# Windowed attention with a gated MLP on one core: second heads of blocks 0 to 2 scaled by GpSimd, first two weight chunks loaded and converted earlier

## The chip, the cores and the metric

One NeuronCore of a Trainium2 chip runs the whole program. The metric is device time in microseconds (us) of one execution; the figure of the kernel before is the median of three runs. A profiled execution of the same program gives the rows that are read below.

## The reference

Inputs are q, k, v of shape (4, 8, 768, 64), two integers n_global (8) and n_local (96), and the weights w_in (512 x 2048) and w_out (2048 x 512). q, k and v are 32-bit floats; the weights come as 64-bit floats and are brought to 32 bits on the chip.

```python
scores = scale * q @ k.T + bias                  # bias = -slope[head] * distance
scores = where(is_global | is_local, scores, -1e9)
a = exp(scores - max(scores)); a = a / (sum(a) + 1e-9)
x = (a @ v) -> (3072, 512)                       # heads side by side
h = x @ w_in;  g = h * sigmoid(h);  out = g @ w_out
```

A query sees the first 8 keys and the 96 keys up to its own position, so a block of 128 queries needs 232 keys: 96 of the block before, 8 global ones, 128 of its own (the first block of each batch needs its own 128 alone).

## The kernel before, in words

**Attention** goes by 24 blocks of 128 queries (4 batches of 6). A block has 4 *pairs* of heads; pair u = 4 * block + hp counts them through. For each pair: TensorE (PE) makes the scores (L625; two pairs in one go in blocks 0 to 5); VectorE (DVE) adds the bias and takes the row maximum, once for each head (L638); ScalarE (ACT) takes the exponential and its row sum (L646); DVE guards and inverts the sum (L653, L657); each head's row is multiplied by the inverse (`norm`, L662 to L668; called *scaling* here); PE turns the rows (L682); ACT moves the turned rows out of PSUM (L692); when the four pairs of a block are there, PE multiplies them with v (L707), ACT casts the result to the high part of x (L725) and DVE takes the low part (L728). In blocks 0 to 2 (pairs 0 to 11) DVE scales both heads of a pair; in pairs 12 to 23 ACT scales the second head (`on_act`, L659, `NA=(12, 24)`).

**The MLP** takes two blocks as a *group* (12 groups). In groups 0 and 1 it goes by 16 steps f: PE makes h (L868, 12 matmuls of 256 columns, of xh and xl with the high and low parts of w_in), ACT and DVE make the gate and its high and low parts (L874, L878, L882, L886), PE multiplies with w_out (L893, 6 matmuls of 512 columns). From group 2 on two steps go together (L971, L1040), by another scheme that the change does not touch.

**The weights** come as 32 chunks n, w_in for even n and w_out for odd n, so that step f needs the chunks 2f and 2f+1. A chunk is loaded by a DMA on SyncE's queue (SP; `stage`, L413), put together from the halves of the 64-bit numbers by three DVE instructions (`conv1` to `conv3`, L415, L421, L427), cast to its high part by ACT (`conv_hi`, L439), and DVE takes the low part (`conv_lo`, L443). The result of the odd chunks also goes back to DRAM from SP's queue (L436).

**The order** is the result of a planner that runs when the kernel is built (`Plan.run`, L102). Every piece of work has an engine, a cost estimate, a *rank*, the pieces that it waits for, and the buffers that it takes. The planner walks through time and gives each free engine the ready piece of the lowest rank. Each engine then executes its list in that order and waits for whatever is not there. In attention, rank is about the pair's number; chunk n is converted at rank `C0 + CR * n` = 14 + n and its load is at one rank less (L447, L449). GpSimd (POOL) has little to do at first: in blocks 0 to 5 it copies columns of k from block to block (L610, L612), and one bias (L339).

Of the kernel before, what the change touches and what calls it, by code (L numbers as in the profile page):

```python
# [17 lines left out]
ALU = mybir.AluOpType  # L18
# [16 lines left out]

    C0=14, CR=1, LW=1, LB=5, QB=3.5, RI=2.8, RN=2.8, RP=0.2, RM=0, RV=1.2, RQ=0.1, RB=3, LK=-25, LAG=1,

    BP=(4, 3), NX=20, CF=8, AHEAD=5, SB=(4,), LQ=(1, 2), CN=3, I0=6, QS='ACT', G0=2, TR=10, RL=4500, TL=6000, CL=3200, VC=8, WT=2, TP=3, ORD=(5, 7, 0, 1, 2, 3, 4, 6), NA=(12, 24), V2=6,
)


# [143 lines left out]
def attn_moe(ctx, tc, q, k, v, n_global, n_local, w_in, w_out, out):  # L185
    nc = tc.nc
# [257 lines left out]

    o_w, o_l, o_raw, o_st = [], [None, None], [], []
    for n in range(2 * NFC):
        rank = PAR["C0"] + PAR["CR"] * n  # L447
        a, m, x = [] if lent(n) is not None else [Buf("big")], Buf("mid", "m"), lent(n)
        o = op("DMA", 1456, rank - PAR["LW"], (lambda n=n: stage(n, "w")), [o_l[x]] if not a else (), a, PAR["DW"])  # L449
        o_st.append(o)  # L450
        o = op("DVE", 335, rank, (lambda n=n: conv1(n)), [o], [*a, m])
        o = op("DVE", 602, rank, (lambda n=n: conv2(n)), [o], [*a, m])
        o = op("DVE", 602, rank, (lambda n=n: conv3(n)), [o], [*a, m])
        if x is not None:
            o_l[x] = o
        o_wf = o
        if n % 2:
            o_raw.append(op("DMA", 800, rank, (lambda n=n: keep_raw(n)), [o], [m], PAR["DO"]))
        hi = op("ACT", 520, rank, (lambda n=n: conv_hi(n)), [o] + (o_l if n >= 2 * NFC - 4 else []), [m])
        lo = op("DVE", 602, rank, (lambda n=n: conv_lo(n)), [hi], [m])  # L460
        o_w.append((hi, lo))
# [197 lines left out]
    def on_act(u):  # L659
        return (1,) if PAR["NA"][0] <= u < PAR["NA"][1] else ()  # L660

    def norm(i, hp, a):  # L662
        t = blk[i]
        x = t["p", hp][:, a, :cols(i)[1]]
        if a in on_act(NHP * i + hp):
            nc.scalar.mul(x, x, t["inv", hp][:, a:a + 1])
        else:
            nc.vector.tensor_scalar(x, x, t["inv", hp][:, a:a + 1], None, ALU.mult)  # L668
# [71 lines left out]
    for i in range(B * NJ):  # L740
# [60 lines left out]
        for hp in range(NHP):  # L801
            u = NHP * i + hp
            stacked = i >= PAR["I0"]
            kind = pt_kind(i, hp)
            pe, pt, tp = Buf("pe", "m"), Buf(kind, "m" if kind == "pt" else None), Buf("tp")
            n = cols(i)[1]
            hps = (hp,) if stacked or (not i and hp < 2) else (hp - hp % 2, hp - hp % 2 + 1)
            if hp == hps[0]:
                s = [Buf("s") for _ in range(1 if stacked else 2)]
                ks = [kk[x] for x in (("KH", "KL", "QH", "QL", "R") if stacked else ("KH", "QH"))]  # L810
                before["s"] = o_s[u] = op(
                    "PE", 440 if stacked else 390 + len(hps) * (385 if j else 218), u,
                    (lambda i=i, hps=hps, s=s: stack_scores(i, hps[0], s) if i >= PAR["I0"] else scores(i, hps, s)),
                    [x for y, x in ob.items() if i or y[1] <= hps[-1] < y[2]] + [before.get("s")], s + ks,
                )
            o = before["s"]
            if not u:
                for x in later:
                    plan.after(x, o)
            if u == PAR["HU"] - 1:  # L820
                o["hold"] = 1
            o_e = []
            for a in range(2):
                x = op("DVE", 318 if j else 210, u, (lambda i=i, hp=hp, a=a: top_of(i, hp, a)),
                       [o, o_b[j == 0, hp], before.get("top") if not a else None], [s[a % len(s)], pe])
                if not a:
                    before["top"] = x
                o_e.append(op("ACT", ACT(n, 112) + 186, u, (lambda i=i, hp=hp, a=a: expo(i, hp, a)), [x], [pe]))
            if i >= PAR["VC"] and hp == 1:
                o_c.append(op("DVE", 598, u + 0.5, (lambda i=i: check_here(i)), [arrived, before["top"]], [kk["vn"]]))  # L830
            o = op("DVE", 67, u - PAR["RI"], (lambda i=i, hp=hp: guard(i, hp)), o_e, [pe])
            o = op("DVE", 72, u - PAR["RI"], (lambda i=i, hp=hp: inverse(i, hp)), [o], [pe])
            o = [op(*(("ACT", ACT(n)) if a in on_act(u) else ("DVE", 250 if j else 196)), u - PAR["RN"], (lambda i=i, hp=hp, a=a: norm(i, hp, a)), [o], [pe])
                 for a in range(2)]
            o = op("PE", 438 if j else 220, u - PAR["RP"], (lambda i=i, hp=hp, tp=tp: turn_p(i, hp, tp)), [*o, joint], [pe, tp])
            o_m.append(op("ACT", ACT(512 if j else 256), u - PAR["RM"], (lambda i=i, hp=hp, pt=pt: move_p(i, hp, pt)), [o, before.get("move")], [tp, pt]))
            before["move"] = o_m[-1]
            pts.append(pt)
# [660 lines left out]
```

## Time and profile before

| what | value |
|---|---|
| runs | 672.61, 673.05, 673.12 us; median 673.05 |
| profiled execution | 673.47 us, of which the span of the trace is 671.7 |
| PE, DVE, ACT, POOL busy | 99%, 81%, 64%, 23% of the span |
| granted TensorE clock | 1.00 of full speed in every slice |
| chain that ended last | PE 94%, DVE 5%, ACT 1% |

The shares of the span are an average over stages. The first 45 us, in which attention runs ahead and the first weights are converted, look different from the rest: there PE has gaps and DVE or ACT hardly any. So the table to read first is the one by stretches of time, and after it each engine's instructions in order of time around the places where PE waits.

### The profile page before, as it was taken

How to read it: one execution, taken by the hardware profiler on the slowest of the kernel's cores; microseconds unless marked ns; L12 is line 12 of the kernel's file. 1: busy time of each engine (PE TensorE's matmuls, PEld its weight loads, DVE VectorE, ACT ScalarE, POOL GpSimd, SP SyncE). 2: the span in 40 equal slices, each digit the busy share in tenths (PEclk: the TensorE clock that was granted, in tenths of full speed). 3: DMA queues.
4: the chain of work that ended last, by engine and by line, in shares of the span. 5: the costliest groups of instructions: out<-in, count | busy, mean ns of one | idle time of the engine just before them, and what ended most of it. 6: DMA issues, size and time to landing. Idle time of an engine off the chain costs nothing.

```text
span 671.7 us, 15715 instructions
## 1 busy us (share of the span) xinstructions
PE 662.1 (99%) x5756; PEld 635.6 (95%) x5756; DVE 543.9 (81%) x1501; ACT 432.2 (64%) x1026; POOL 156.2 (23%) x345
## 2 busy tenths in 40 slices
PE   8999999999999999999999999999999999999997
PEld 6788999899999999999999999999999999999997
DVE  6999999998668888878878878877879887975545
ACT  6997544687567676665775766674767666663332
POOL 2100000010003322324323323323332322332331
PEclk9999999999999999999999999999999999999999
DMA  9997757575887589669577677675876788744451
GB/s 183 223 292 246 235 165 232 180 236 181 237 248 249 167 261 280 199 178 297 190 222 237 196 213 219 206 234 171 281 220 191 224 229 212 234 161 153 129 190 34
DMA packets 146067, 141.62 MB, mean 211 GB/s; under 512 B 88356, under 2 KB 115492, under 8 KB 145988
## 3 DMA queue, kind: packets, MB, share of 16 engines
q1 hardware_dynamic: 145984, 140.60, 70.3%
q8 instruction: 46, 0.75, 0.5%
q14 instruction: 33, 0.27, 0.1%
q10 hardware_dynamic: 4, 0.00, 0.0%
HBM read 117.44 MB, written 18.87 MB: 203 GB/s over the span
## 4 chain that ended last, share of the span: by engine, by line
PE 94%; DVE 5%; ACT 1%; issue 0%; DVEq 0%; ACTq 0%
PE bank L971 33%; PE bank L1040 29%; PE bank L893 7%; PE bank L868 6%; PE bank L707 5%; PE bank L682 5%; PE bank L595 5%; PE bank L527 3%; DVE pe L638 1%; DVE pe L668 1%; PE bank L625 1%; PE bank L1312 0%; ACT pe L646 0%; DVE wf L427 0%; DVE wf L421 0%; DVE ost L1072 0%
## 5 line engine op out<-in xcount | busy, mean ns | idle before, releaser
L989 POOL TENSOR_TENSOR sg<-sg 128x128 f32<-128x128 f32 x285 | 131.1, 481 | 285.3 <-DVE sg L983 232.5
L971 PE MATMUL bank<-xh,WIH 128*128 128x256 f32 x640 | 183.2, 286 | 0.0
L971 PE MATMUL bank<-xl,WIH 128*128 128x256 f32 x640 | 177.9, 278 | 0.0
L971 PE MATMUL bank<-xh,WIL 128*128 128x256 f32 x640 | 177.7, 278 | 0.0
L1011 DVE TENSOR_TENSOR gl<-sg,gh 128x512 fp32r<-128x512 f32 (+1 forms) x152 | 98.2, 651 | 37.9 <-ACT gh L1005 34.1
L971 PEld LDWEIGHTS bank<-xl,WIH 128*128 128x128 f32 x640 | 120.7, 189 | 0.5
L971 PEld LDWEIGHTS bank<-xh,WIH 128*128 128x128 f32 x640 | 120.7, 189 | 0.4
L971 PEld LDWEIGHTS bank<-xh,WIL 128*128 128x128 f32 x640 | 120.4, 188 | 0.0
L1005 ACT CAST gh<-sg 128x512 fp32r<-128x512 f32 (+1 forms) x152 | 84.0, 568 | 54.1 <-PE bank L1040 40.3
L646 ACT ACTIVATE pe<-pe,NM 128x232 f32<-128x232 f32 (+1 forms) x192 | 90.2, 473 | 36.7 <-DVE NM L638 35.9
L977 ACT ACTIVATE sg<-bank 128x512 f32<-128x512 f32 x80 | 47.7, 597 | 47.8 <-PE bank L971 47.3
L638 DVE CUSTOM_DVE_ANT_0 pe<-bank,B 128x232 f32<-128x232 f32 (+1 forms) x192 | 66.6, 374 | 12.8 <-PE bank L595 11.7
L1040 PE MATMUL bank<-WOH,gh 128*128 128x256 f32 (+1 forms) x280 | 73.8, 295 | 0.0
L983 DVE SCALAR_TENSOR_TENSOR sg<-sg,bank 128x512 f32<-128x512 f32 x80 | 54.8, 685 | 23.5 <-ACT sg L977 22.9
L1040 PE MATMUL bank<-WOL,gh 128*128 128x256 f32 (+1 forms) x280 | 72.3, 289 | 0.0
L668 DVE TENSOR_SCALAR pe<-pe,sm 128x232 f32<-128x232 f32 (+1 forms) x180 | 60.5, 371 | 1.4
L682 PE MATMUL bank<-ident,pe 128*128 128x128 f32 (+1 forms) x352 | 55.0, 276 | 3.7 <-DVE pe L668 3.5
L692 ACT COPY pt<-bank 128x512 f32<-128x512 f32 (+1 forms) x82 | 44.7, 549 | 15.5 <-PE bank L682 13.4
L1040 PEld LDWEIGHTS bank<-WOH,gh 128*128 128x128 f32 x280 | 52.8, 189 | 1.5 <-issue 0.7
L1040 PEld LDWEIGHTS bank<-WOL,gh 128*128 128x128 f32 x280 | 52.7, 188 | 0.8
L1040 PE MATMUL bank<-WOH,gl 128*128 128x256 f32 (+1 forms) x280 | 49.0, 292 | 0.0
L682 PEld LDWEIGHTS bank<-ident,pe 128*128 128x128 f32 (+1 forms) x352 | 39.9, 136 | 9.0 <-DVE pe L668 6.1
(165 smaller groups left out, 1511.0 us busy)
## 6 DMA issues: line engine op xcount, KB each, us to landing
tx<-ts SPq DMA_DIRECT2D x72, 512.0 KB
ty<-ts SPq DMA_DIRECT2D x72, 256.0 KB
c<-in_moe_w_in_dram SPq DMA_DIRECT2D x16, 512.0 KB
c<-in_moe_w_out_dram SPq DMA_DIRECT2D x16, 512.0 KB
vn<-in_v_dram SPq DMA_DIRECT2D x24, 256.0 KB
w<-in_moe_w_in_dram SPq DMA_DIRECT2D x12, 512.0 KB
w<-in_moe_w_out_dram SPq DMA_DIRECT2D x12, 512.0 KB
kn<-in_k_dram SPq DMA_DIRECT2D x23, 256.0 KB
```

What stands on the lines that cost most here:

```text
L638: nc.vector.tensor_tensor_reduce(t["p", hp][:, a, :n], t["s", hp][a][:, :n], B1[:, hp] if i % NJ else B0[:, hp], -SC / (1 + a), 3.0e38, AL ...
L646: nc.scalar.activation(x, x, AF.Exp, bias=NM[:, i * H + h:i * H + h + 1], scale=-1.0, accum_out=t["sum", hp][:, a:a + 1],)
L668: nc.vector.tensor_scalar(x, x, t["inv", hp][:, a:a + 1], None, ALU.mult)
L682: nc.tensor.transpose(ps[:n, c, a], pe[:, a, c0:c0 + n], ident)
L893: nc.tensor.matmul(po, a[:, s], w_o(w, f), start=f == 0 and n == 0, stop=f == NFC - 1 and n == 2)
L971: nc.tensor.matmul(ph[:, a], w[:, cc, fs], x[:, cc], start=not cc and not m, stop=cc == NCC - 1 and m == 2)
L977: nc.scalar.activation(x[:, 0:4].rearrange("p (a b) c -> p a (b c)", a=2), mo["ph", g, n], AF.Tanh, scale=0.5)
L983: nc.vector.scalar_tensor_tensor(x, x, 1.0, mo["ph", g, n], ALU.add, ALU.mult)
L989: (eng.tensor_sub if e else eng.tensor_add)(x[:, o], x[:, a], x[:, b])
L1005: nc.scalar.copy(mo["gh", g, n][:, a:b], mo["sg", g, n][:, a + o:b + o])
L1011: nc.vector.tensor_sub(mo["gl", g, n][:, a:b], mo["sg", g, n][:, a + o:b + o], mo["gh", g, n][:, a:b].bitcast(F32))
L1040: nc.tensor.matmul(o, l, r, start=(g, b) not in opened, stop=n == NFC // 2 - 1 and m == 2 and (p in ((2, 7, 5, 4) if g == NGRP - 1 else (6 ...
```

## The change

It does two things. First, in pairs 0 to 11 the second head (a = 1) is scaled by GpSimd instead of DVE, with a planner cost of 450 (128 keys) or 650 (232 keys). Second, chunks 0 and 1 get ranks of their own: the load is at rank 0.3 (before: 13 and 14) and the conversion at rank 8 and 8.1 (before: 14 and 15); rank 8 is where pair 8, the first of block 2, stands. All other ranks stay, and lines behind L660 move down by 1 to 5. The number of instructions on PE stays.

```diff
-    BP=(4, 3), NX=20, CF=8, AHEAD=5, SB=(4,), LQ=(1, 2), CN=3, I0=6, QS='ACT', G0=2, TR=10, RL=4500, TL=6000, CL=3200, VC=8, WT=2, TP=3, ORD=(5, 7, 0, 1, 2, 3, 4, 6), NA=(12, 24), V2=6,
+    BP=(4, 3), NX=20, CF=8, AHEAD=5, SB=(4,), LQ=(1, 2), CN=3, I0=6, QS='ACT', G0=2, TR=10, RL=4500, TL=6000, CL=3200, VC=8, WT=2, CE=8, LE=0.3, NP=(0, 12), TP=3, ORD=(5, 7, 0, 1, 2, 3, 4, 6), NA=(12, 24), V2=6,
...
-        rank = PAR["C0"] + PAR["CR"] * n
+        rank = PAR["C0"] + PAR["CR"] * n if n > 1 else PAR["CE"] + n / 10
...
-        o = op("DMA", 1456, rank - PAR["LW"], (lambda n=n: stage(n, "w")), [o_l[x]] if not a else (), a, PAR["DW"])
+        o = op("DMA", 1456, rank - PAR["LW"] if n > 1 else PAR["LE"], (lambda n=n: stage(n, "w")), [o_l[x]] if not a else (), a, PAR["DW"])
...
+    def on_pool(u, a):
+        return a == 1 and PAR["NP"][0] <= u < PAR["NP"][1]
+
     def norm(i, hp, a):
         t = blk[i]
         x = t["p", hp][:, a, :cols(i)[1]]
-        if a in on_act(NHP * i + hp):
+        if on_pool(NHP * i + hp, a):
+            nc.gpsimd.tensor_scalar(x, x, t["inv", hp][:, a:a + 1], None, ALU.mult)
+        elif a in on_act(NHP * i + hp):
...
-            o = [op(*(("ACT", ACT(n)) if a in on_act(u) else ("DVE", 250 if j else 196)), u - PAR["RN"], (lambda i=i, hp=hp, a=a: norm(i, hp, a)), [o], [pe])
+            o = [op(*(("POOL", 650 if j else 450) if on_pool(u, a) else ("ACT", ACT(n)) if a in on_act(u) else ("DVE", 250 if j else 196)), u - PAR["RN"], (lambda i=i, hp=hp, a=a: norm(i, hp, a)), [o], [pe])
```

The planner makes a new order of it on every engine. It differs from the old one in the first stage alone: from the middle of group 2 on, PE's order is the same row for row. Three places matter to what follows.

SP's queue, from the q of block 2 on. kn, qn and vn are the loads of k, q and v of a block (kn_307 and kn_379 are block 3's, vn_394 and vn_393 block 2's, qn_351 and qn_415 block 3's), vp what a block keeps of the block before. Before:

```order
L513 DMA qn_287<-in_q_dram 128x8x64
L513 DMA kn_307<-in_k_dram 128x8x64
L521 DMA vp_333<-vn_232 96x512
L522 DMA vp_333<-vp_274 8x512
L513 DMA qn_351<-in_q_dram 128x8x64
L513 DMA kn_378<-in_k_dram 128x8x64
L513 DMA vn_394<-in_v_dram 128x8x64
```

And with the change:

```order
L513 DMA qn_287<-in_q_dram 128x8x64
L411 DMA w_0_309<-in_moe_w_in_dram 128x4x256
L411 DMA w_1_340<-in_moe_w_out_dram 128x1024
L521 DMA vp_367<-vn_232 96x512
L522 DMA vp_367<-vp_274 8x512
L513 DMA kn_379<-in_k_dram 128x8x64
L513 DMA vn_393<-in_v_dram 128x8x64
L513 DMA qn_415<-in_q_dram 128x8x64
```

The two chunks stand ahead of the k of block 3, and the q of block 3 now stands behind the v of block 2, which waits until block 0 is done with its buffer.

ACT's queue up to the cast of block 3's result (xh_616 from bank4_113 before, xh_649 from bank1_110 now; it makes group 1 ready). wf are converted chunks on the way to their high part, ths and ghs the gate of a step f and its high part, pe the rows of a pair. Before:

```order
L882 CAST ghs_125<-ths0_127 128x256
L600 ACTIVATE QHw_695<-bank2_111,few_121 128x512
L692 COPY pt_700<-bank1_110 128x512
L439 CAST WIH_104<-wf_2_653 128x4x128
L646 ACTIVATE pe_702,sm_703<-pe_702,NM_108 128x232 x2
L646 ACTIVATE pe_731,sm_732<-pe_731,NM_108 128x232 x2
L666 ACTIVATE pe_702<-pe_702,sm_703 128x232
L725 CAST xh_616<-bank4_113 128x4x128
```

And with the change:

```order
L697 COPY pt_729<-bank0_109 128x512
L600 ACTIVATE QHw_734<-bank7_116,few_121 128x512
L439 CAST WOH_106<-wf_3_674 128x512
L879 ACTIVATE ths0_127<-bank2_111 128x256
L671 ACTIVATE pe_687<-pe_687,sm_688 128x232
L646 ACTIVATE pe_719,sm_720<-pe_719,NM_108 128x232 x2
L887 CAST ghs_125<-ths0_127 128x256
L730 CAST xh_649<-bank1_110 128x4x128
```

Chunk 3's high part (before: the row behind the cast of block 3), the gate of step 1 and its high part now stand ahead of it; all else that ACT does up to there is the same in number.

PE's queue at the first matmul of group 1 (the row that reads xh_616 before, xh_649 now). Before, with the rows of pair 17 (pe_731) just turned:

```order
L682 MATMUL bank0_109<-ident_99,pe_731 104x128 x2
L682 MATMUL bank0_109<-ident_99,pe_731 128x128 x2
L868 MATMUL bank3_112<-xh_391,WIH_104 128x256
L868 MATMUL bank3_112<-xl_400,WIH_104 128x256
L868 MATMUL bank3_112<-xh_391,WIL_105 128x256
L868 MATMUL bank3_112<-xh_391,WIH_104 128x256
L868 MATMUL bank3_112<-xl_400,WIH_104 128x256
L868 MATMUL bank3_112<-xh_391,WIL_105 128x256
L868 MATMUL bank4_113<-xh_616,WIH_104 128x256
```

And with the change, where pair 17 is pe_719:

```order
L898 MATMUL bank3_112<-WOH_106,ghs_125 128x512
L898 MATMUL bank3_112<-WOL_107,ghs_125 128x512
L898 MATMUL bank3_112<-WOH_106,gls_126 128x512
L873 MATMUL bank7_116<-xh_649,WIH_104 128x256
L873 MATMUL bank7_116<-xl_665,WIH_104 128x256
L873 MATMUL bank7_116<-xh_649,WIL_105 128x256
L873 MATMUL bank7_116<-xh_649,WIH_104 128x256
L873 MATMUL bank7_116<-xl_665,WIH_104 128x256
L873 MATMUL bank7_116<-xh_649,WIL_105 128x256
L687 MATMUL bank2_111<-ident_99,pe_719 104x128 x2
```

Up to the turn of pair 17 PE had 18 matmuls L868 and 3 L893 of group 0 before; up to group 1's first matmul it now has 24 and 9, while pair 17 is turned behind it. The rest of what lies ahead is the same in number.

## Rows read from the trace of the kernel before

**Rows 1.** Stretches of time: start and end, length, busy us by engine, clock, DMA.

```profile
core 0: us, PE busy (x) PEld busy (x) DVE busy (x) ACT busy (x) POOL busy (x), PEclk, DMA share, GB/s
0.00:10.70 10.70, 9.35 (x46) 7.27 (x47) 5.78 (x33) 4.76 (x12) 2.84 (x15) 1.00 0.92 169
10.70:28.00 17.30, 16.21 (x154) 12.91 (x155) 15.33 (x90) 17.18 (x61) 2.04 (x6) 1.00 0.87 207
28.00:44.10 16.10, 13.50 (x138) 10.87 (x136) 16.07 (x60) 15.66 (x47) 1.17 (x2) 1.00 1.02 276
44.10:662.00 617.90, 617.90 (x5386) 599.75 (x5384) 501.44 (x1309) 392.08 (x905) 148.90 (x320) 1.00 0.70 212
662.00:671.70 9.70, 5.14 (x43) 4.75 (x41) 5.28 (x13) 2.50 (x5) 1.29 (x2) 1.00 0.18 57
```

**Rows 2.** Chain that ended last, around 78 us: start, length, work.

```profile
77.73 2.09 PE bank L893 x9
79.82 1.41 PE bank L868 x12
```

**Rows 3.** Instructions in order of time, PE: start, length, what; turn of pair 17.

```profile
44.87 0.81 PE L682 MATMUL bank<-ident,pe 128*104 128x128 f32 x4
45.43 0.36 PE L868 MATMUL bank<-xh,WIH 128*128 128x256 f32 x1
```

**Rows 4.** In order of time, DVE: low part of block 3's result.

```profile
44.55 0.71 DVE L728 TENSOR_TENSOR xl<-bank,xh 128x512 fp32r<-128x512 f32 x1
```

**Rows 5.** In order of time, ACT: four rows back to back.

```profile
47.42 0.62 ACT L439 CAST WIH<-wf 128x512 fp32r<-128x512 f32 x1
47.94 0.40 ACT L882 CAST ghs<-ths 128x256 fp32r<-128x256 f32 x1
48.25 0.37 ACT L874 ACTIVATE ths<-bank 128x256 f32<-128x256 f32 x1
48.52 0.48 ACT L666 ACTIVATE pe<-pe,sm 128x232 f32<-128x232 f32 x1
```

**Rows 6.** In order of time, DVE: conversion and scaling back to back.

```profile
36.27 0.40 DVE L415 TENSOR_SCALAR wf<-w 128x512 uint32<-128x512 uint32 x1
36.60 0.33 DVE L668 TENSOR_SCALAR pe<-pe,sm 128x232 f32<-128x232 f32 x1
36.85 0.67 DVE L443 TENSOR_TENSOR WOL<-wf,WOH 128x512 fp32r<-128x512 f32 x1
37.45 0.15 DVE L653 TENSOR_SCALAR sm<-sm 128x2 f32<-128x2 f32 x1
```

**Rows 7.** In order of time, POOL: a bias, and a copy without DVE conversions beside it.

```profile
6.85 0.56 POOL L339 TENSOR_SCALAR B<-t 128x128 bf16<-128x128 f32 x1 [4.63 <-DVE t L314]
...
13.04 0.21 POOL L610 COPY KHw<-KHw 128x32 f32<-128x32 f32 x1 [0.91 <-PE bank L625]
```

**Rows 8.** In order of time, POOL: copies with DVE conversions beside them.

```profile
29.78 0.72 POOL L610 COPY KHw<-KHw 128x32 f32<-128x32 f32 x1 [6.95 <-PE bank L625]
30.45 0.50 POOL L612 COPY KHw<-KHw 128x384 f32<-128x384 f32 x1
```

**Rows 9.** In order of time, DVE: the conversions beside those copies.

```profile
29.74 0.69 DVE L421 SCALAR_TENSOR_TENSOR wf<-w,wf 128x512 uint32<-128x512 uint32 x1
...
30.47 1.02 DVE L427 SCALAR_TENSOR_TENSOR wf<-w,wf 128x512 uint32<-128x512 uint32 x1
```

**Rows 10.** In order of time, DVE: maximum of pair 11's second head.

```profile
23.97 0.39 DVE L638 CUSTOM_DVE_ANT_0 pe<-bank,B 128x232 f32<-128x232 f32 x1
```

**Rows 11.** In order of time, ACT: exponential of pair 11's second head.

```profile
25.88 0.50 ACT L646 ACTIVATE pe<-pe,NM 128x232 f32<-128x232 f32 x1
```

**Rows 12.** In order of time, SP's DMA issues: q of block 3, v of block 2.

```profile
14.02 0.43 SPq L513 DMA_DIRECT2D qn<-in_q_dram  x1
...
18.01 0.37 SPq L513 DMA_DIRECT2D vn<-in_v_dram  x1
```

**Rows 13.** In order of time, PE: q of block 3, and the turn of pair 7.

```profile
19.97 0.60 PE L527 MATMUL bank<-ident,qn 128*128 128x128 f32 x4
...
22.13 0.80 PE L682 MATMUL bank<-ident,pe 128*128 128x128 f32 x4
```

## The prediction

> **What bounds the kernel now.** I read the stretches of time first [rows 1]. From 44.1 to 662 us PE is busy in 617.90 of 617.90 us; its pace there is the end of the program, and behind 662 us stands a tail that the change doesn't touch. So what can be won lies ahead of 44.1 us. There PE is idle for 1.35 us up to 10.7 us (the start), 1.09 us up to 28 us and 2.60 us up to 44.1 us: 3.69 us in the two stretches in which the change works. In the same stretches ACT is idle for 0.12 and 0.44 us, DVE for 1.97 and 0.03 us. So PE waits for ACT and DVE there, and ACT is the tighter one: it has 0.56 us in 33.4 that nothing fills.
>
> From this a way to price the change follows. Once group 1 can be worked on, PE has two groups to choose from and doesn't stop any more. What counts is **how much PE work is done when that point comes, and how late it comes**. In the old trace the turn of pair 17 gives way to the next matmul at 45.43 us [rows 3]; the low part of block 3's result, the last thing that group 1 needs, is there at 44.55 + 0.71 = 45.26 us [rows 4]. I take these two for the comparison.
>
> **The work that is done by then.** By the order shown above, PE had 18 L868 and 3 L893 by 45.43 us; now it has 24 and 9 ahead of group 1's first matmul. One L893 takes 2.09 / 9 = 0.232 us and one L868 1.41 / 12 = 0.118 us on a PE that does not wait [rows 2]. So 6 x 0.232 + 6 x 0.118 = 2.10 us more are done. The turn of pair 17 is still to come, 45.43 - 44.87 = 0.56 us [rows 3]. **Net 1.54 us ahead.**
>
> **How late the point comes.** ACT now does one chunk's high part, one gate and one gate's high part more ahead of the cast of block 3. Back to back these take 0.52, 0.27 and 0.31 us (47.42 to 47.94, 48.25 to 48.52, 47.94 to 48.25 [rows 5]). **1.10 us later**, with ACT as full as before. DVE is no closer: up to block 3's low part its list holds one conversion more (0.33 for L415 and three of 0.60 like L443, 2.13 in all) and a gate and its low part (about as long as L415 each, 0.66), and 13 scalings fewer, 13 x 0.25 = 3.25 (36.60 to 36.85) [rows 6], so it gets some 0.5 us shorter.
>
> **The sum without new waits:** 45.43 - (45.26 + 1.10) + 1.54 = 0.61 us gained. To that comes w, what ACT waits more (or less) than before on its way there.
>
> **What the second head on GpSimd costs.** DVE gives up 12 scalings of 0.25 us. POOL's time for one is not in the old trace. From below: a copy of 384 columns takes 0.50 us [rows 8], so one of 232 no more than that by this row. From above: the multiplication of 128 columns for a bias takes 0.56 us [rows 7], which for 232 would be 1.0 us. I take some 0.7 us, between the two, as it is a multiplication with a scalar but of 32 bits all through. The turn waits for both heads, so it can come up to 0.75 us later than now. In pairs 4 to 11 this is hidden: ACT is full, and the turned rows wait for their place in its list. If that cover is gone, each pair costs up to 0.75 us. In pairs 1 to 3 ACT's list has little else between, and a few tenths can show.
>
> **What it does to DVE.** When POOL copies while DVE converts, both get slower: the copy of 32 columns takes 0.72 instead of 0.21 us [rows 7, 8] beside an L421 that runs from 29.74 us, and the L427 from 30.47 us takes 1.02 us beside the next copy, against 0.69 for the L421 ahead of it [rows 8, 9]. So one meeting costs DVE 0.33 us. Up to the maximum of pair 11's second head DVE's list now has two conversions more (4.26 us) and nine scalings fewer (2.25 us): 2.0 us longer. About ten of POOL's scalings fall into that time. If every one met a conversion or a first head's scaling at 0.33 us, DVE would lose 3.3 us more. Against that stand the 1.97 us of idle DVE time [rows 1] and the lead of that maximum over the exponential that reads it, 25.88 - (23.97 + 0.39) = 1.52 us [rows 10, 11]. So half of the meetings are free, all of them cost ACT 2.0 + 3.3 - 1.97 - 1.52 = 1.8 us. From below nothing: no meeting at all. The Trainium skill ("SBUF — State Buffer", section "SBUF: two separate sides") states that GpSimd and a DVE instruction with two SBUF inputs share one pair of ports as an exclusive lock for a whole instruction, and the loser blocks. The trace agrees that one waits for the other. By that rule the loss per meeting could be a whole POOL instruction, ten times 0.7 us instead of 3.3, and the end some 3.7 us later than with 0.33 each.
>
> **The loads.** The two chunks move from behind block 5's k to ahead of block 3's k on SP's queue. They are asked for ahead of 14.02 us, the old place of block 3's q [rows 12], and their conversion stands behind pair 5's scaling, so I take them to be there in time (C prices the other case). What they push back is: the q of block 3, asked for at 14.02 us, now comes behind the v of block 2, which was free to go at 18.01 us [rows 12]. It was used 19.97 - 14.02 = 5.95 us after its issue [rows 12, 13], which bounds its way from above; so it is there by 18.01 + 0.37 + 5.95 = 24.3 us. Its turn now stands behind that of pair 7, which ran at 22.13 us [rows 13]. So PE waits between 0 and about 1.6 us; I take 0, since 5.95 us includes lying about. The store of chunk 1 now holds back the k of block 5, which PE turns only behind block 2's product with v; nothing.
>
> **w.** From below: all of ACT's 0.56 us of waits vanish. From above 1.8 us (every meeting). I take +0.2 us, near the lower end, because DVE's free time covers the first half of the meetings. **Gain 0.61 - 0.2 = 0.4 us.** The profiled execution would take 673.47 - 0.4 = 673.1 us. The median of the runs shown lies 0.42 us below the profiled one, so it goes from 673.05 to **672.6 us**. With the ends of w: 671.9 to 674.2 us.
>
> A measurement of this kernel can tell about 0.2%, 1.35 us, from no change: faster is below 671.7, slower above 674.4 us. The forecast case and its bounds lie in between.
>
> **Rivals.**
>
> *A. The meetings on GpSimd and DVE decide; slower.* Place: pairs 6 to 11, where chunks 0 and 1 are converted between the scalings. If a meeting costs DVE not 0.33 but 0.56 us, the whole of POOL's shortest multiplication [rows 7], it is 2.0 + 5.6 - 3.49 = 4.1 us that ACT waits, and the end is 672.6 - 0.2 + 4.1 = 676.5; at 0.4 us it is 674.9. It decides from about 0.35 us a meeting on. For it: the 0.72 us copy lost 0.51, more than the 0.33 [rows 7, 8]. Against it: not each scaling meets something, and POOL may be the one that waits. Chance 0.17. The lock that the Trainium skill states ("SBUF — State Buffer", section "SBUF: two separate sides") puts the loss at up to the whole instruction of the other engine; by that rule A would come ahead of the other rivals.
>
> *B. ACT is not the limit; faster.* The ACT rows overlap and may hide waits, and then DVE's list (0.5 us shorter) sets the point. Then it comes 0.5 us earlier instead of 1.10 later, the gain is 45.43 - 44.76 + 1.54 = 2.2 us, and the median 670.8 us. For it: in the second stretch DVE is idle for 0.03 us only, ACT for 0.44 [rows 1]. Against it: ACT's work up to there is 1.10 us more, and it has 0.56 us to spare. Chance 0.17.
>
> *C. The loads decide.* The q of block 3 comes 1.6 us late or the first chunk lands late and holds DVE: 672.6 + 1.6 = 674.2 us, at the border. Chance 0.08.
>
> *D. The work only changes places.* PE gets step 0 early, and waits as much later for step 2: no change, 673.0 us. Against it: every conversion from chunk 2 on stands 3 us earlier in DVE's list (twelve scalings fewer). Chance 0.1, part of "same".
>
> **How the numbers follow.** Forecast case 0.48, A 0.17, B 0.17, C 0.08, D 0.1. Faster by over 0.2%: B and 0.05 of the forecast case (the points of comparison are set by hand), 0.22. Slower: A and a part of C, 0.20. Within: 0.58. The range holds the forecast's bounds, D and C, most of A's lower half and a part of B: 671.1 to 674.9 us.
>
> **What would show it.** In the profile of the changed kernel: PE idle from 10.7 us to where it stops being idle at some 3.3 us instead of 3.69, and the first matmul of group 1 at 46.4 to 46.6 us; step 0's matmuls ahead of the turn of pair 10; ACT idle by at most a few tenths in between; POOL scalings of 0.5 to 1.0 us; PE without idle time from then on to 662 us. A first matmul of group 1 at 47.5 us or later with waits of ACT for DVE's maxima speaks for A, one at 45 us for B, a PE that waits at the q of block 3 for C, new gaps of PE behind 46 us for D. Wrong altogether would be a span whose difference lies behind 46 us.

## The result, and the profile after

The changed kernel takes 677.39 us (median of 4 runs, 676.41 to 677.93) against 672.92 us of the kernel before (672.61 to 673.12): the ratio is 1.0064, with a 95% interval of 1.0052 to 1.0076. That is 4.5 us slower, outside the range of 671.1 to 674.9 us. Run again, beside 15 runs of the kernel before on one chip, it took 676.92 against 673.04 us, ratio 1.0055 (1.0041 to 1.0069).

The page of the changed kernel puts the profiled run of 676.41 us at a span of 671.5 us; before, the profiled run of 673.47 us had a span of 671.7. So the span did not grow, and the time *around* it did: from 1.8 to 4.9 us. I call a run's own time less its span its **outside time**. In all runs of the kernel before it is 1.73 to 1.84 us; in the four of the changed kernel 4.91, 4.97, 4.71 and 5.23 us, with spans of 671.5, 672.9, 672.2 and 672.7. The median of the spans is 672.45 here; in 14 later runs of the kernel before, beside the first experiments, it was 671.15. So some 3.1 us of the 4.5 lie outside, some 1.3 inside.

What lies behind the span is seen in the view of the DMA queues, from 671.7 to 680 us. The kernel before has one line there, and nothing moves:

```profile
DMA packets 0, 0.00 MB, mean 0 GB/s; under 512 B 0, under 2 KB 0, under 8 KB 0
```

The changed kernel, same stretch:

```profile
DMA packets 5, 0.05 MB, mean 6 GB/s; under 512 B 0, under 2 KB 0, under 8 KB 0
## 3 DMA queue, kind: packets, MB, share of 16 engines
q8 instruction: 1, 0.02, 1.3%
q14 instruction: 4, 0.03, 1.2%
```

Five blocks of instructions, one of 16 KB and four of 8 KB, are fetched there. In the trace they start 2.8 to 3.1 us behind the end of the span, and the last lands at 676.3 us from its start.

Inside the span, the stretches [rows 1] after the change (start and end, length, busy us by engine, clock, DMA):

```profile
core 0: us, PE busy (x) PEld busy (x) DVE busy (x) ACT busy (x) POOL busy (x), PEclk, DMA share, GB/s
0.00:10.70 10.70, 8.19 (x50) 5.81 (x52) 5.47 (x33) 4.97 (x12) 3.58 (x16) 1.00 0.93 169
10.70:28.00 17.30, 14.75 (x140) 11.01 (x137) 16.39 (x77) 16.72 (x58) 9.75 (x13) 1.00 0.95 212
28.00:44.10 16.10, 15.66 (x155) 13.26 (x153) 15.06 (x61) 16.01 (x49) 3.26 (x7) 1.00 1.08 279
44.10:662.00 617.90, 617.79 (x5383) 599.24 (x5382) 499.88 (x1308) 391.11 (x907) 147.83 (x320) 1.00 0.70 212
662.00:671.70 9.70, 4.97 (x41) 4.57 (x40) 5.28 (x13) 2.40 (x5) 1.29 (x2) 0.97 0.18 57
```

PE's idle time in the second and third stretch is now 2.55 and 0.44 us. What ended it, from 9 us on (engine, line, releaser: us, times, longest):

```profile
PE bank L527 <- DMA kn<-in_k_dram: 1.2, 1, 1.2
PE bank L527 <- DMA qn<-in_q_dram: 0.8, 1, 0.8
PE bank L625 <- ACT QHw L600: 0.5, 2, 0.3
PE bank L687 <- POOL pe L669: 0.2, 1, 0.2
```

Before, DVE's scalings ended 3.5 us of PE's waits and no DMA any. Now k and q of block 3 come late: 2.0 us. SP's issues tell why k does (start, length):

```profile
11.52 0.59 SPq L411 DMA_DIRECT2D w<-in_moe_w_in_dram  x1
12.15 0.50 SPq L411 DMA_DIRECT2D w<-in_moe_w_out_dram  x1
...
14.12 0.38 SPq L513 DMA_DIRECT2D kn<-in_k_dram  x1
```

Before, this k was asked for at 11.61 us:

```profile
11.61 0.58 SPq L513 DMA_DIRECT2D kn<-in_k_dram  x1
```

POOL's scalings, by shape (busy us, mean ns; idle before):

```profile
L669 POOL TENSOR_SCALAR pe<-pe,sm 128x232 f32<-128x232 f32 x8 | 7.8, 979 | 6.4 <-DVE sm L657 3.0 <-ACT pt L697 1.6 <-PE bank L687 0.7
...
L669 POOL TENSOR_SCALAR pe<-pe,sm 128x128 f32<-128x128 f32 x4 | 2.8, 712 | 3.8 <-DVE B L339 1.7 <-DVE sm L657 1.6 <-DVE sm L653 0.5
```

**Two executions at different paces.** The two profiled executions can't be laid on each other as they are. Ahead of 10 us the same four turns of q take 1.11 us in the one of before and 0.66 in the one of after (PE in order of time, first before, then after):

```profile
8.51 1.11 PE L527 MATMUL bank<-ident,qn 128*128 128x128 f32 x4
```

```profile
8.42 0.66 PE L527 MATMUL bank<-ident,qn 128*128 128x128 f32 x4 [0.54 <-DMA qn<-in_q_dram]
```

The stretches show a granted clock of 1.00 for both, and so does the table ahead of the prediction ("in every slice"). But the trace's clock records begin only at 10.1 us before and at 5.5 us after; ahead of its first record the view prints 1.00 without one. Up to there a turn starts every 0.21 us, behind it every 0.11, and four turns that fall into a stretch recorded at 0.50 (p5, at 23.3 us) take 1.09 us. So the figure of 1.00 is wrong for the start: TensorE ran there at the pace of the lower of its clock's two levels, 1.2 GHz. Six profiled executions in the order of the kernel before (before and the runs e4, p1, p3, p4 and s1 below) differ by idle instructions or small copies alone. With the full pace from 4.1 us on the span is 670.9 us (e4), from 5.4 us 671.0 (p3), from 9.4 us 671.4 (s1), from 9.9 to 10.1 us 671.5 to 671.7 (p4, p1, before). So the moment at which TensorE comes to its pace moves this kernel by 0.8 us; why it differs no run tells. A second profiled execution of the changed kernel (r1) comes to it late, at 10.3 us, as the profiled one of before; its span is 672.9 us.

### The profile page after: what moved, and what is told of

It is laid out like the page before. It is cut to its first block, busy times and chain, and to the rows that moved or that the text cites. A ratio compares the mean times of both kernels' runs of the same rounds, so it can differ in the third digit from the quotient of the medians.

```text
span 671.5 us, 15735 instructions
## 1 busy us (share of the span) xinstructions
PE 661.4 (98%) x5756; PEld 633.9 (94%) x5756; DVE 542.1 (81%) x1489; ACT 431.2 (64%) x1026; POOL 165.7 (25%) x357
## 4 chain that ended last, share of the span: by engine, by line
PE 94%; DVE 4%; ACT 2%; issue 1%; DVEq 0%; ACTq 0%
PE bank L976 33%; PE bank L1045 29%; PE bank L898 7%; PE bank L873 6%; PE bank L712 5%; PE bank L687 5%; PE bank L595 5%; PE bank L527 2%; DVE pe L638 1%; ACT pe L646 1%; PE bank L625 1%; PE bank L1317 0%; DVE pe L673 0%; DVE sm L653 0%; DVE ost L1077 0%
## 5 line engine op out<-in xcount | busy, mean ns | idle before, releaser
L673 DVE TENSOR_SCALAR pe<-pe,sm 128x232 f32<-128x232 f32 (+1 forms) x168 | 58.3, 379 | 1.6
L1045 PE MATMUL bank<-tx,gh 128*128 128x256 f32 x288 | 45.8, 278 | 0.0
```

The costliest lines, as they stand in the source:

```text
L1045: nc.tensor.matmul(o, l, r, start=(g, b) not in opened, stop=n == NFC // 2 - 1 and m == 2 and (p in ((2, 7, 5, 4) if g == NGRP - 1 else (6 ...
```

## Experiments: the parts, each alone

**Only the scalings** (e1): the ranks of chunks 0 and 1 as before.

```diff
-        rank = PAR["C0"] + PAR["CR"] * n if n > 1 else PAR["CE"] + n / 10
+        rank = PAR["C0"] + PAR["CR"] * n
-  ..., rank - PAR["LW"] if n > 1 else PAR["LE"], ...
+  ..., rank - PAR["LW"], ...
```

> Only the twelve scalings on GpSimd; the two weight chunks are loaded and converted as in the kernel before. The changed kernel's 4.5 us lie mostly outside its span (a run's own time less its span is 4.9 us, 1.8 us before), where five instruction packets land 2.8 us behind the end of the span, and none before. Theory T (the length of GpSimd's instruction list: 12 more on it move its end, and with that something has to be fetched at the end): outside 4.9 us, those five packets there, total 676 to 678 us. Rival W (the moved weights and the order of loads on SP carry it): outside 1.8 us, total 672.5 to 673.5 us. Inside the span, if the scaling alone makes the gain of the first blocks: span 671.0 to 671.8 us.

Measured 676.51 us, outside 1.8, span 674.7 us (medians). **Only the weights** (e2):

```diff
-    ..., NP=(0, 12), ...
+    ..., NP=(0, 0), ...
```

> Only the two chunks loaded and converted early; all scalings on the engines of before. Theory T (length of GpSimd's list) and rival I (the scaling instruction itself, on GpSimd): outside the span 1.8 us, no instruction packet behind the span, total 672 to 674 us. Rival W (weights and load order): outside 4.9 us, total 676 to 678 us. Inside: k and q of a later pair land late as in the changed kernel (2.0 us of waits of TensorE there), so without the scaling's relief a span of 671.7 to 673.7 us.

Measured 675.93 us, outside 1.8, span 674.1. **One scaling** (e3), e1 with one pair:

```diff
-    ..., NP=(0, 12), ...
+    ..., NP=(11, 12), ...
```

> One scaling alone on GpSimd (pair 11's second head), weights as before: GpSimd's list is one instruction longer instead of twelve. Rival I (the scaling on GpSimd brings a fixed cost outside the span, whatever their number): outside 4.9 us. Theory T (length of the list): outside 1.8 us unless that one instruction already passes the point, then 4.9 us; the five packets behind the span must go with it either way. Rival W: outside 1.8 us. Span 671.4 to 672.0 us in each.

Measured 680.16 us, outside 1.8, span 678.35. **Twelve fills in place of the scalings** (e4), in the kernel before:

```diff
+        if a == 1 and NHP * i + hp < 12:
+            nc.gpsimd.memset(late, 0)
         if a in on_act(NHP * i + hp):
```

> The kernel before, with twelve fills of one element on GpSimd at the places of the scalings, and nothing else changed: 12 x 0.1 us on an engine that is busy 23 % of the span, which nobody waits for. Theory T (length of GpSimd's list): outside the span 4.9 us and five instruction packets behind it, total 676 to 677 us with a span of 671.5 to 671.9 us. Rivals I (the scaling itself) and W (weights): outside 1.8 us, total 672.6 to 673.5 us.

Measured 672.94 us, outside 1.8, span 671.15: no change.

None of the four has the outside time, so neither part brings it by itself, and theories T, I and W fall in the form in which they were put. The spans teach something else: each part alone is *worse inside* than both together. The order is planned anew for each, and what the plan does further back is no part of the edit. With one scaling moved, the one wait that stands out is this, at 145 us, a hundred us behind the scaling (e3, waits of PE from 60 us on):

```profile
PE bank L976 <- DVE xl L733: 3.5, 1, 3.5
```

Behind it the granted clock is low for 8 us (0.58, 0.50, 0.50 and 0.71 in the stretches of 2 us from 147 to 155 us), which takes another 3.4 us of TensorE's pace; both together are most of what this span is longer. Where e1 and e2 lose theirs stays open.

So parts of such a change can't be added up, and what follows keeps an order and edits one thing in it.

## Experiments: the same order, one thing edited

**The changed kernel again** (r1).

> The changed kernel word for word, once more, beside runs of the kernel before on the same chip. Theory K (the 3.1 us outside the span belong to the kernel: something in this very program has to be fetched once more at its end): outside the span 4.9 us again with five instruction packets behind the span, total 676.4 to 678 us. Rival L (they belong to that one loading of the program onto a chip, not to the program): outside 1.8 us, none of the five packets, total 673.3 to 674.8 us from spans of 671.5 to 673.

Measured 676.92 us, outside 4.8, span 672.1: theory K, the outside time belongs to the program. **The twelve scalings on VectorE, at the same places** (r2):

```diff
-            nc.gpsimd.tensor_scalar(x, x, t["inv", hp][:, a:a + 1], None, ALU.mult)
+            nc.vector.tensor_scalar(x, x, t["inv", hp][:, a:a + 1], None, ALU.mult)
```

> The changed kernel's order of every engine and its loads, but the twelve scalings run on VectorE at the same places of the order. If GpSimd's relief of VectorE is what shortens the first 44 us: the twelve scalings put 12 x 0.2 to 0.25 us = 2.4 to 3.0 us back on VectorE, less the scalings on GpSimd being 0.5 us slower each: span 0.5 to 2 us longer than the changed kernel's of the same chip. If the relief is worth nothing because GpSimd takes 0.7 to 0.98 us where VectorE takes 0.2 to 0.35 us: span 0 to 1 us shorter. Outside the span: 4.9 us if that belongs to this order, 1.8 us if to the GpSimd instructions or to the one loading.

Measured 674.13 us, outside 1.8, span 672.35. **k of block 3 ahead of the chunks** (r3):

```diff
     def stage(n, nm):
+        if nm == "w" and n == 0:
+            load(3, "k")
...
     def load(i, nm, h0=0, h1=H):
+        if i == 3 and nm in blk[i]:
+            return
```

> The changed kernel, but the load of k of block 3 is issued ahead of the two chunks instead of behind them. Theory C (the chunks ahead of k on SP hold up TensorE and the first stretch): the wait of TensorE for that load, 1.2 us, is gone and the span is 0.5 to 1.2 us shorter than the changed kernel's. Rival (VectorE and ScalarE end the stretch whatever TensorE waited for): the wait is gone and the span stays within 0.3 us. Outside as in the changed kernel, whichever that is.

Measured 676.87 us, outside 5.0, span 671.8 (4 runs), and no wait of PE for k or q in its profile. That is 0.3 us shorter than r1's span (5 runs), less than single runs differ by, so the rival holds: the wait goes and the span stays. In the place of k, at 21.4 us, PE waits 0.8 us for VectorE's row sums (L653 in the kernel before). **Block 0 alone on GpSimd** (p2):

```diff
-            nc.gpsimd.tensor_scalar(x, x, ...)
+            (nc.vector if i else nc.gpsimd).tensor_scalar(x, x, ...)
```

> The changed kernel's order, with block 0's four scalings on GpSimd and those of blocks 1 and 2 (232 columns, 0.87 to 1.19 us each on GpSimd) on VectorE at the same places. GpSimd's list is 8 scalings and their waits shorter than the changed kernel's. Theory P: outside 1.8 us. Rival S: SyncE's list is some 2 instructions shorter too, so it would allow either. Inside: if a scaling of 232 columns on GpSimd is what keeps TensorE and ScalarE waiting, the span is 0.3 to 0.8 us shorter than the changed kernel's 672.1; if GpSimd's relief of VectorE counts more, as long as that of the run with all twelve on VectorE (672.35) or up to 0.3 us longer.

Measured 673.76 us, outside 1.8, span 672.0. With the edit of r3 on top (p5):

> The two edits together that each shortened the changed kernel: block 0's scalings alone on GpSimd, and k of block 3 loaded ahead of the two chunks. Outside 1.8 us. If the wait for k and the scalings of 232 columns each cost their own 0.1 to 0.3 us of span, 671.4 to 671.8 us of span and a total of 673.2 to 673.6 us, level with the kernel before; if the first stretch is ended by the same work on VectorE and ScalarE in each, 672.0 us of span and 673.8 us as with the first edit alone.

Measured 673.88 us, outside 1.8, span 672.1: the two edits don't add.

## Experiments: what is fetched behind the program

The outside time comes and goes with what stands in the lists, so I counted all records of each engine in the traces, waits and branches among them. GpSimd runs 377 before and 405 after, SyncE 686 and 690. First, lists made longer in the kernel before, GpSimd by 36 (p1), VectorE by 24 (p4), SyncE by 10 copies of four bytes (p3), each in the middle of the program:

```diff
-        for emit in order:
+        for m, emit in enumerate(order):
+            if 2600 <= m < 2636:
+                nc.gpsimd.memset(late, 0)
             emit()
```

> The kernel before, with 36 fills of one element on GpSimd in the middle of the program, on which nobody waits (36 x 0.03 to 0.1 us = 1 to 4 us on an engine idle for three quarters of the span). It makes GpSimd's list as long as the changed kernel's (which runs 405 instructions there, waits counted; before 377; the scalings alone 403). Theory P (GpSimd's list, once longer than some point between 403 and 405 instructions, is what has the five blocks fetched behind the program): outside the span 4.9 us, five instruction packets behind it, total 675.8 to 676.8 us from a span as before, 671 to 672 us. Rival S (SyncE's list, 690 instructions in the changed kernel, at most 687 in those without the cost): 1.8 us, total as before. Rival Z (the five lists together, 9979 in the changed kernel, at most 9972 in those without; here 9995): 4.9 us.

> The kernel before, with 24 fills of one element on VectorE in the middle of the program (24 x 0.06 us), where VectorE is busy four fifths of the time and TensorE does not wait for it. The five lists together hold 9983 instructions, GpSimd's 377 and SyncE's 686 as before. Rival Z (the sum of the lists): outside 4.9 us and five packets behind the span. Theory P and rival S: 1.8 us and none. Span 671 to 672.5 us in each.

> The kernel before, with ten copies of four bytes from memory to memory, issued by SyncE in the middle of the program and waited for by nobody; SyncE's list grows by them and their waits, past the changed kernel's 690 instructions. Rival S (the length of SyncE's list, 690 in the two kernels with the cost, at most 689 in the others, is what has the five blocks fetched behind the program): outside the span 4.9 us and five instruction packets behind the span, total 676 to 677 us. If outside stays at 1.8 us, neither GpSimd's list nor SyncE's nor their sum is the cause by its length alone, and what it is stays open. Span 671 to 672 us in each (ten issues of 0.3 to 0.5 us on SyncE, which is not busy there).

Measured 673.33, 673.17 and 673.28 us, outside 1.8 in all three: not the length as such. What was left was an exact length. s1 is p1 with 28 fills, s2 the changed kernel with 10 of them, s3 is p3 with 4 copies (s1, p1 and the kernel before differ in GpSimd's list alone):

> The kernel before with 28 fills of one element on GpSimd in the middle of the program: GpSimd runs 405 instructions, as in the changed kernel; SyncE 686. Theory G (GpSimd's list ends at the edge of a block at 405; at 403 it ends ahead of it, at 413 behind it): outside the span 4.9 us and five packets behind it, total 676 to 677 us. Rival Y (SyncE's list at 690) and rival B (only both parts together): 1.8 us, total 672.8 to 673.5 us.

> The changed kernel with ten fills of one element more on GpSimd in the middle of the program: 415 instructions there, SyncE's 690 as in the changed kernel. Theory G: outside 1.8 us and none of the packets, total 673.6 to 674.6 us from a span of 671.8 to 672.8. Rivals Y and B: 4.9 us, total 676.7 to 677.7 us.

> The kernel before with four copies of four bytes more on SyncE: 690 instructions there, GpSimd's 377. Rival Y (SyncE's list ends at the edge of a block at 690; 689 is ahead of it, 696 behind it): outside 4.9 us and five packets, total 676 to 677 us. Theory G and rival B: 1.8 us, total 672.8 to 673.5 us.

**s1 took 676.31 us: the kernel before, with nothing added but 28 fills that nobody waits for, is 3.2 us slower** (ratio 1.0044, 1.0031 to 1.0058), at a span of 671.5 us, and outside 4.7. Its DMA queues behind the span, 671.7 to 680 us:

```profile
q14 instruction: 4, 0.03, 1.2%
q8 instruction: 1, 0.02, 1.1%
```

s2, the changed kernel with ten instructions *more*, took 674.16 us: outside 1.8, span 672.35. By GpSimd's records, over all the kernels:

```
GpSimd records   kernels                      outside us
377 to 386       before, e2, e3, e4, r2, p2,  1.8
                 p3, p4, p5, s3
403              e1                           1.8
404              s4                           1.8 to 2.0 (6 runs), 4.8 to 5.1 (4)
405              after, r1, r3, s1            4.7 to 5.2 (one 5.6)
413, 415         p1, s2, t1                   1.8
```

SyncE's 690 is in s2 and s3 without the cost, so rival Y falls, and so does B: s1 has neither part of the change. Theory G stands: it is where GpSimd's list ends. Lengths of 387 to 402 and 406 to 412 were not tried. In p1 and s2 there are two 8 KB packets more than before, one of them at the program's end, 1.0 and 1.2 us ahead of the end of the span, and none behind it: by the look of it the block that is missing at 405 records is there by then. The Trainium skill ("Runtime: NRT & Kernel Launch", section "Instruction fetch mechanics") states that each engine's list streams in through blocks, in sequence, and that crossing a block's edge is mostly hidden. The trace agrees on the blocks (packets of 16 and 8 KB); on the edge the measurement decides: in p1 and s2, whose lists are longer, it costs nothing, and where the list ends at 405 records it costs 3 us (at 404 in 4 of 10 runs). Why five blocks are fetched then, and not one, no run tells.

s3 has a loss of its own. It took 675.61 us at an outside time of 1.8: its span is 673.85. In the profile 2.0 of the 2.4 us lie behind the last arithmetic. This copy ends the work in each (DVE in order of time, before and s3); the span ends 3.2 us behind its start at 671.7 us before, and 5.2 us behind it at 674.1 us in s3:

```profile
668.52 0.13 DVE L1319 COPY late<-bad 1x1 int32<-1x1 int32 x1
```

```profile
668.92 0.13 DVE L1322 COPY late<-bad 1x1 int32<-1x1 int32 x1
```

In its trace SyncE waits 1.80 us for VectorE there, whose list has 1733 records instead of 1732. That this is the same thing at an edge of VectorE's list, inside the span, is a guess that no run tried.

**The scaling alone, in the old order** (s4). The kernel before with its order kept, second heads of blocks 0 to 2 on GpSimd:

```diff
+        if a == 1 and NHP * i + hp < 12:
+            nc.gpsimd.tensor_scalar(x, x, t["inv", hp][:, a:a + 1], None, ALU.mult)
-        if a in on_act(NHP * i + hp):
+        elif a in on_act(NHP * i + hp):
```

> The kernel before in its own order of every engine, but the second heads' scalings of blocks 0 to 2 run on GpSimd at the same places: no replanned order, no early weights. If the scaling on GpSimd (0.7 us at 128 columns, 0.9 to 1.2 us at 232) delays the turns of the pairs by what it is longer than on VectorE, since the order leaves it no lead: 12 x 0.3 to 0.7 us of waits of TensorE, most of it ahead of 44 us, span 672.5 to 676 us. If VectorE's relief (12 x 0.2 to 0.35 us) makes up for it: 671 to 672 us. Outside 1.8 us unless GpSimd's list ends at 404 to 412 instructions (theory G), then 4.9 us may come.

Measured 675.3 us, span 672.4 against 671.4; outside on the fence, as the table shows. So without the new order the scaling on GpSimd costs 1.0 us inside, just under the first expectation (672.5 to 676). In 4 of its 10 runs the granted clock is below 0.998, against 2 of 27 of the kernel before; the median of the other six is 672.05, so some 0.4 us of it come by the clock. PE waits for DVE's scalings for 3.1 us as before, and for POOL's 0.5.

## Experiments: what is left inside

For the inside I summed, over the matmuls of a trace, what each one's slot (from its start to the next one's) is longer than the median slot of its kind behind 60 us in the kernel before; a shorter one counts against it. This sees stretched matmuls too, which the busy share hides. It leaves out the 34 matmuls of the first 11 us whose kind doesn't come again, and with them the 0.8 us of the pace, so that before and e4 end level.

```
us lost by TensorE up to      50      150     200     the end   pace comes
before                        11.30   13.86   14.46   20.96     late
s1 (before with 28 fills)     11.21   13.77   14.37   20.86     late
e4 (before with 12 fills)     11.22   13.83   14.44   20.93     early
p3 (before with 10 copies)    11.37   13.93   14.54   21.03     early
r1 (the change)               10.86   13.16   14.43   22.09     late
r3 (the change, k first)      11.00   13.39   14.66   21.10     late
after (the change)            11.33   13.57   14.84   21.34     early
s2 (the change, 10 fills)     13.77   16.23   17.49   24.36     early
```

Three readings. At equal pace (r1 and before) the change is 0.44 us ahead at 50 us and 0.70 at 150. Between 150 and 200 us every kernel with the new order gives 1.3 us away, before 0.6: the lead is gone. Of the 0.7 us that this is more, L595 has 0.4, and 0.27 of that is one place where PE stands still, at 155 us in after, r1 and r3 and nowhere before: VectorE writes KL of a later block until 154.99 us, and the load of it into PE begins at 155.10 (after, in order of time, L580 on DVE and L595). The profile names no releaser there ("issue"), so that it waits for KL is read from the times alone:

```profile
154.30 0.69 DVE L580 SCALAR_TENSOR_TENSOR KL<-bank,KL 64x512 fp32r<-64x512 f32 x1
155.10 0.19 PEld L595 LDWEIGHTS bank<-KL,QL 128*128 128x128 f32 x1 [0.26 <-issue]
```

From 200 us on after loses 6.5 us, as before does; r1 has 1.2 us more, 0.8 of it for one late q at 478 us. And where the pace comes early (after beside p3 and e4) there is no lead at 50 us: PE gets to the work of the first stretch sooner, and it is not there. In after that is k and q of block 3; in t1 below, with k asked for first, it is VectorE's work.

How late k and q are varies. In s2's profile, a span of 674.5 us, PE waits 1.7 us for the k of block 3 and 1.9 for its q (the rest of the first line is an early q at 8.8 us, for which e4 waits as well):

```profile
PE bank L527 <- DMA qn<-in_q_dram: 2.5, 2, 1.9
PE bank L527 <- DMA kn<-in_k_dram: 1.7, 1, 1.7
```

Its stretches from 20 to 32 us (columns as above):

```profile
20.00:22.00 2.00, 0.58 (x5) 0.58 (x6) 2.00 (x9) 1.79 (x7) 1.69 (x2) 1.00 1.16 205
22.00:24.00 2.00, 0.95 (x9) 0.71 (x7) 2.00 (x9) 1.40 (x3) 2.00 (x4) 1.00 0.71 152
24.00:26.00 2.00, 1.11 (x14) 0.97 (x16) 1.99 (x9) 1.09 (x4) 0.58 (x1) 1.00 0.83 203
26.00:28.00 2.00, 2.00 (x23) 2.00 (x21) 1.18 (x6) 1.70 (x6) 0.00 (x0) 0.50 0.81 199
28.00:30.00 2.00, 2.00 (x14) 1.40 (x14) 1.01 (x2) 0.93 (x2) 0.91 (x1) 0.64 0.05 13
30.00:32.00 2.00, 2.00 (x21) 1.71 (x18) 1.24 (x8) 2.00 (x9) 0.40 (x1) 1.00 0.98 247
```

PE is busy for 2.64 of 6 us, and then the granted clock stands at 0.50 and 0.64, of which 0.50 is the lower of its two levels, 1.2 GHz. That takes some 2 x 0.50 + 2 x 0.36 = 1.7 us of its pace. The granted clock of a whole run tells which runs had such a stretch: below 0.998 it is in 2 of the first 4 runs of the change and none of r1's 5, in 4 of 10 of s2 and 4 of 11 of t1 (spans of 672.4 to 674.8 us), and in 4 of 113 of the kernel before. That late loads bring it is seen in s2's profile alone. In p5's, with k first, the granted clock is 0.51 from 23.2 to 26.6 us behind waits of 0.8 and 0.6 us for VectorE and 0.3 for q, and t1 has k first as well; so an earlier k doesn't keep the slow stretches away.

The last run takes the outside time and the late k away (t1): r3 with ten fills.

> The changed kernel with k of block 3 loaded ahead of the two chunks and ten fills of one element more on GpSimd (415 instructions there). Theory G: outside 1.8 us. Inside, if the late k and q are the loss in the span (waits of TensorE of 1.0 to 4.2 us in the runs of the changed order, none in the kernel before): span 671.2 to 671.6 us, level with the kernel before, and no run near 674. If the replanned order behind them costs as well (0.6 us more lost by TensorE between 150 and 200 us): span 671.7 to 672.1 us, total 673.5 to 673.9 us.

Measured 673.82 us, outside 1.8, span 672.0 against 671.4. So the second expectation: the replanned order keeps about 0.6 us. No load of block 3 is waited for in its profile; PE waits 0.6 us each for an early k and q, at 7.3 and 8.5 us, as it does in e4. At 21.4 us, where after waits for k, PE now waits for VectorE's row sum (waits of PE; the lines of t1 are 4 further than those of after):

```profile
PE bank L691 <- DVE sm L657: 1.2, 1, 1.2
```

The first matmul of group 1 comes at 46.60 us, in r3 at 46.82, no earlier than after's 46.45. So the late k covered a wait for VectorE of much the same length. No variant of the change beat the kernel before; the nearest was p2, 673.76 us, ratio 1.0010 (1.0000 to 1.0020).

## Why the prediction was wrong

- **The step that failed** is the last of the sum: "The median of the runs shown lies 0.42 us below the profiled one, so it goes from 673.05 to 672.6 us." It carries a difference of spans over to the time, and so takes what lies around the span as fixed. It was not: 1.8 us became 4.9. 28 idle fills do the same (s1), ten more undo it (s2). No row of before shows it; the count of GpSimd's records was there, but not where a block ends. Without this the change would have stood at 674.2 us (s2), inside the range, and been called the same by the bound of 0.2%.
- **Where the difference would lie:** "Wrong altogether would be a span whose difference lies behind 46 us." By that sentence it was wrong: most of it lies behind the span, and the lead of the first stretch is lost between 150 and 200 us. "PE without idle time from then on to 662 us" fails at 155 us. L595 has 0.4 of the 0.7 us lost there and the turns (L682) 0.3, the latter in slots a little longer, without one cause that I could show. Rival D (the work only changes places) comes nearest to it, though at another place.
- **The lead** was right in its mechanism and size, at the pace of the run it was made on. "Gain 0.61 - 0.2 = 0.4 us": r1, which comes to its pace late like the profiled execution of before, is 0.44 us ahead at 50 us. ACT stayed as full as forecast: it is idle for 0.5 to 0.7 us from 10.7 to 44.1 us in after, r1, r3 and t1 (0.56 before). The first matmul of group 1 was put at 46.4 to 46.6 us; it came at 46.45 (after) and 46.59 (r1). In after (PE in order of time; the second row is the turn of pair 17, as in [rows 3]):

```profile
46.45 0.28 PE L873 MATMUL bank<-xh,WIH 128*128 128x256 f32 x1
...
47.15 0.60 PE L687 MATMUL bank<-ident,pe 128*104 128x128 f32 x4
```

- But a profile was taken for *the* pace. Where the pace comes early, the kernel before passes the point of [rows 3] at 44.55 instead of 45.43 us (e4), and the changed one still comes to its own at 46.45 (after) and, with no load of block 3 to wait for, at 46.60 (t1).
- **The loads** were mis-sized. "I take 0" for q, at most 1.6 us: PE waited for q 0.4 to 1.9 us. The k of block 3 was not priced at all, though two chunks of 512 KB go ahead of it: 0.6 to 1.7 us. In after and r1 this cost little, since with k first PE waits for VectorE instead (t1, r3); in s2's profile it moved the rest of the program by 2.7 us against after, some 1.7 of them by the clock (the estimate above), which no term had. Rival C had this place at 0.08 and 674.2 us. That s2's median of 674.16 meets it is luck: t1, with k first, stands at 673.82.
- **GpSimd's scaling** takes 0.71 us for 128 columns and 0.98 for 232, so the estimate of 0.7 was low and the upper bound of 1.0 held. PE waited 0.2 us for one. That moving it off VectorE is worth anything in this order is not shown: the median spans of s2 and r2 are 672.35 both. Among the runs whose granted clock stayed at 0.998 or above s2's is 671.95 (6 runs) and r2's 672.35 (8), but s2 has twice as many of the others. In the old order it costs 1.0 us (s4).
- **Rivals A and B** did not come: from 9 to 46.5 us ACT waits for DVE's maxima 0.2 us at most (after, r1, r3, t1), and there is no point at 45 us. Nothing here shows the exclusive lock deciding the time.

## What to carry to other kernels

Price the run, not the span: compare a run's own time less its span before and after, and if it has moved, look for instruction packets behind the end before looking for a cause in the work. A few idle instructions more on that engine are a cheap trial, and a change that adds or takes instructions should be judged with its list ending clear of an edge. Where several transfers share an issuing queue, price every one that is pushed back by the moved ones, ask what TensorE would wait for next if the load were there, and what its idle time costs after the wait as well as in it.

## What the runs showed that I had not expected

- 28 fills of one element, 2.5 us in all on an engine idle for three quarters of the time, make a kernel of 673 us 3.2 us slower, and 36 of them don't. At 404 records one and the same program ended either way: 1.8 to 2.0 us outside in six runs, 4.8 to 5.1 in four.
- The pace of TensorE's first 10 us differs from execution to execution: the clock records of the traces begin, and the turns double their pace, between 4.1 and 10.8 us. The views print 1.00 ahead of that. It moves the span of this kernel by about 0.8 us.
- With 2.64 us of work in 6 us behind it, TensorE's granted clock was at 0.50 for 2 us and at 0.64 for 2 more (s2). The waits that came before were for data that had been asked for later than in the kernel before; so this late load was paid for twice.
- Taking the wait for k away left a wait for VectorE of 0.8 to 1.2 us at the same place (r3, t1). What an engine waits for last hides what it would wait for next.
